# A two-term VectorE exponential, fixed PSUM slots, column-tiled FFN matmuls and a new planner in an attention-plus-FFN kernel

## The chip, the cores and the metric

The kernel runs on one core of a Trainium2 chip. A core has TensorE (PE: matmuls, with weight loads shown apart as PEld), VectorE (DVE), ScalarE (ACT), GpSimd (POOL), SyncE (SP, which here issues DMAs) and 16 DMA engines. Matmuls write into PSUM, which has 8 banks of 128 partitions x 512 fp32 values; TensorE reads its operands from SBUF. The metric is the device time of one execution in microseconds. For the kernel before it is 923.64 us, the median of 3 runs (923.12 to 926.92).

## The reference

The input x has 2048 tokens of 512 features in bf16. It is normalised, and the normalised xn goes through two branches:

```
xn = layernorm(x)                              # 2048 x 512
q = xn @ wq   (32 heads of 16)                 # 2048 x 512
k, v = xn @ wk, xn @ wv                        # one k and one v of 2048 x 16 for all heads
s = softmax(q k^T / 4) v, all heads, @ wo      # 2048 x 512
g = silu((silu(xn @ w_gate) * (xn @ w_up)) @ w_down)   # inner width 1792
out = x + s * g
```

The heavy part is the softmax: 32 heads x 2048 queries x 2048 keys give 134 million exponentials.

## The kernel before

**Tiles.** Heads are taken in 4 groups of 8 (`NQ`), and queries in 4 chunks of 512 (`NSC`). A *pair* is one group of heads on one query chunk: 16 pairs. Of a pair's 8 heads, 4 are computed in one *block* (`half` 0 or 1): 32 blocks. A block goes over 16 key tiles of 128 keys (`NT`), and each key tile is split in two *score tiles* (x = 0, 1) of two heads each. So there are 1024 score tiles, each 128 keys x 1024 (2 heads x 512 queries) in fp32: two PSUM banks.

**Scores.** A score tile is two matmuls (L771 to L776) with 32 contraction rows each; x = 0 uses row groups 0 and 1 of the array, x = 1 uses 2 and 3. They go into one of three slots of two banks, `ring[0..2]` (L338; `ring_96` to `ring_98` in the profile). Any slot serves either engine; the planner takes the one that comes free first (L757 to L769).

**Exponentials.** Most tiles go to ScalarE: one activation from the slot into a bf16 buffer `Pb` (L793; 8 buffers). Some go to VectorE, two tiles at a time, which builds the exponential from the bits of a fixed-point sum: a first pass from the slot to 16-bit integers `Ub` (L824, once per tile), then on both tiles together a mask for the mantissa `Wb` (L836), a mask for the exponent `Eb` (L839), a product Wb x Wb (L842) and a product Wb x Ub (L845). Three terms, `Eb`, `Ub` and `Wb`, each weighted by its own copy of v (`VD`, three copies), add up to the probability.

**PV.** Probabilities times v go into the one bank `o_ps` (L665), as four matmuls on the four 32-column groups of the array: one group of four for two ScalarE tiles (L813), three groups for a VectorE pair (L849 to L852). v carries a column of ones, so the sums of the softmax come out too. At the end of a block VectorE copies `o_ps` to SBUF (L708); four small DMAs, a reciprocal (L633), two DMAs and a product on GpSimd (L644) normalise a pair.

**FFN.** Everything else on TensorE goes through the one bank `m_ps`, as full 128 x 128 matmuls: per query chunk 14 column blocks with 4 gate matmuls (L563), a tanh on ScalarE (L568), silu on VectorE (L570), 4 up matmuls, and a product on VectorE (L574); then 4 token tiles of 14 down matmuls (L583) with a tanh (L589) and a product (L591). So do the q projections of later pairs (`g_q`, L547) and the output projections (`g_out`, L613).

**The order of the work.** The builder plans it in Python with a list scheduler (`_Sched`, L177 to L266) that holds a cost for each operation, a latency of 0.13 us between engines and 0.09 us for a change of the array's tile shape. The loop at L737 goes over key tiles in order; for each it fixes the slots and which tile, if any, VectorE takes (only while its planned backlog is under 4.0 us, `D_BL`, L751 to L755), adds the operations, and steps the plan until the scores are placed. FFN, q and output jobs join at fixed tile counts (`gates`, L680 to L691) with matmuls in bundles of two. In the end all operations are emitted by planned start, chained in that order on every engine (`chain`, L477; L869 to L872). The first part (statistics, normalisation, transposes, k and q of the first 512 tokens, L456 to L472) stands ahead of the plan and is not chained; k and v of tokens 512 to 2047 (`g_prolog`, L526) are in the plan. After the last block come the output projection of the last chunk and a check of ranges (L874 to L903).

Of the kernel before, what the change touches and what calls it, by code (L numbers as in the profile page):

```python
# [9 lines left out]
BF16 = mybir.dt.bfloat16  # L10
# [16 lines left out]
CE, CS, CM = 0.45803766, 0.46571725, 4.0 * 0.07629173  # L27
DEN_LO = 16.0
DEN_HI = 1e30
V_HI = 60000.0  # L30

# [135 lines left out]
class _Op:  # L167
    __slots__ = ("eng", "dur", "deps", "emit", "mode", "prio", "name", "start", "end", "left", "users", "ready", "seq")
# [8 lines left out]
class _Sched:  # L177
    LAT = 0.13
    SWITCH = 0.09
    SAME = {"DVE": 0.08, "POOL": 0.08}  # L180
    GUARD = {"PE": 2.0, "DVE": 0.2}

    def __init__(self, t0):
        self.free = {"PE": t0, "ACT": t0, "DVE": t0, "POOL": t0, "DMA": 0.0}
        self.ready = {e: [] for e in self.free}
        self.done = []
        self.seq = 0
        self.mode = None
        self.last_pe = None
        self.backlog = {e: 0.0 for e in self.free}  # L190

    def add(self, op):
        op.seq = self.seq
        self.seq += 1
        self.backlog[op.eng] += op.dur
        op.left = 0
        for d in op.deps:
            if d.start is None:
                d.users.append(op)
                op.left += 1  # L200
# [3 lines left out]

    def _arm(self, op):
        r = 0.0
        for d in op.deps:
            lat = self.LAT if d.eng != op.eng else self.SAME.get(op.eng, 0.0)
            r = max(r, d.end + lat)
        op.ready = r  # L210
        self.ready[op.eng].append(op)

    def _sw(self, o):
        return self.SWITCH if o.eng == "PE" and self.mode is not None and o.mode[0] != self.mode else 0.0

    def _pick(self, e):
# [3 lines left out]
        t = self.free[e]  # L220
        if e == "DMA":
            op = min(lst, key=lambda o: (o.ready, o.seq))
            return op.ready, op
        tm = max(t, min(o.ready for o in lst))
        best = min((o for o in lst if o.ready <= tm + 1e-9), key=lambda o: (o.prio, o.seq))
        if e in self.GUARD:
            hot = [o for o in lst if o.prio[0] <= 0 and o.ready > tm]
            if hot and best.prio[0] > 0:
                h = min(hot, key=lambda o: (o.ready, o.seq))
                lim = h.ready + self.GUARD[e]  # L230
                fit = [o for o in lst if o.ready <= tm + 1e-9 and tm + o.dur + self._sw(o) <= lim]
# [3 lines left out]
    def step(self):  # L235
        cand = None
        for e in self.free:
            c = self._pick(e)
# [698 lines left out]
```

## Time and profile before

| what | value |
|---|---|
| median of 3 runs | 923.64 us (923.12 to 926.92) |
| span of the profiled execution | 922.9 us |
| TensorE busy | 787.4 us (85%) in 5769 matmuls |
| VectorE busy | 709.9 us (77%) in 849 instructions |
| ScalarE busy | 822.8 us (89%) in 920 instructions |
| GpSimd busy | 58.1 us (6%) |
| mean granted TensorE clock | 0.914 |
| first exponential on ScalarE starts | 20.77 us |

All rows but the first are of the one profiled execution, whose own time from first to last instruction is 922.9 us. A group or timeline row reads: start and duration in us (or the group's busy time and the mean ns of one), engine, line, operation, output<-inputs by the program's names, shapes, and how many; square brackets hold the engine's idle time just before and what ended it. Instructions on one engine overlap at their ends, so the cost of one in a full queue is the distance from its start to the next start, not its duration. The granted clock is 1.0 or 0.5 at any one time.

### The profile page before, as it was taken

The numbers are of one execution on the slowest core, as the hardware profiler recorded it, in microseconds if no ns is written. First come the engines' busy times: TensorE is split into PE (matmuls) and PEld (weight loads), VectorE is DVE, ScalarE is ACT, GpSimd is POOL, SyncE is SP. The second block draws the span as 40 slices with busy tenths as digits, with TensorE's granted clock in tenths as the row PEclk, the third lists the DMA queues.
The fourth block names the chain that finished last, engine by engine and source line by source line (L and its number), as shares of the span: only waits on it lengthen the run. The fifth ranks groups of instructions, "written<-read, shape, count | busy, mean of one in ns | idle before, by whom it ended". The sixth has DMA issues, their size and how long they took to land.

```text
span 922.9 us, 14837 instructions
## 1 busy us (share of the span) xinstructions
PE 787.4 (85%) x5769; PEld 231.2 (25%) x5769; DVE 709.9 (77%) x849; ACT 822.8 (89%) x920; POOL 58.1 (6%) x64
## 2 busy tenths in 40 slices
PE   3799888889989898889989888898988889999960
PEld 1222222222222222222222222222222222222210
DVE  6426798887777768898879889888788778697763
ACT  2688899999899999999999999999999999899850
POOL 2100000000000110000001010000000020000001
PEclk9856799899799999999999999989999999799775
DMA  9100000000000000000000000000000000000001
GB/s 332 46 1 1 19 1 20 1 1 19 1 20 7 28 9 1 20 2 19 1 19 8 19 18 1 20 1 19 1 19 7 10 27 1 19 2 19 1 4 41
DMA packets 20110, 18.64 MB, mean 20 GB/s; under 512 B 9024, under 2 KB 15936, under 8 KB 20032
## 3 DMA queue, kind: packets, MB, share of 16 engines
q1 hardware_dynamic: 18448, 17.05, 6.1%
q8 instruction: 47, 0.77, 0.3%
q10 hardware_dynamic: 1584, 0.56, 0.2%
q14 instruction: 31, 0.25, 0.1%
HBM read 12.88 MB, written 2.36 MB: 17 GB/s over the span
## 4 chain that ended last, share of the span: by engine, by line
PE 43%; ACT 25%; DVE 19%; issue 8%; DMA 3%; SPq 2%; POOL 0%; ACTq 0%; DVEq 0%; POOLq 0%
PE o_ps L665 11%; PE m_ps L563 7%; PE ring_98 L772 6%; PE ring_97 L772 6%; PE ring_96 L772 5%; DVE Ub_129 L824 4%; PE m_ps L583 4%; DVE Ub_130 L824 4%; ACT Pb_125 L793 3%; ACT Pb_126 L793 3%; ACT Pb_122 L793 3%; ACT Pb_128 L793 3%; ACT Pb_121 L793 3%; ACT Pb_124 L793 3%; ACT Pb_123 L793 3%
## 5 line engine op out<-in xcount | busy, mean ns | idle before, releaser
L772 PEld LDWEIGHTS <-KT_84 32*128 32x128 bf16 x1024 | 51.0, 92 | 193.9 <-issue 186.9
L772 PEld LDWEIGHTS <-KT_85 32*128 32x128 bf16 x1024 | 50.3, 92 | 181.5 <-issue 179.1
L563 PE MATMUL m_ps<-xnT,wg_sb 128*128 128x512 bf16 x224 | 70.1, 415 | 5.4 <-DVE hT L574 2.0
L563 PE MATMUL m_ps<-xnT,wu_sb 128*128 128x512 bf16 x224 | 69.5, 404 | 4.0 <-DVE ab_137 L570 2.4
L583 PE MATMUL m_ps<-wd_sb,hT 128*128 128x512 bf16 x224 | 67.7, 391 | 5.5 <-DVE g_sb L591 5.4
L824 DVE TENSOR_SCALAR Ub_129<-ring_98 128x1024 uint16<-128x1024 f32 x37 | 45.2, 1223 | 31.9 <-PE ring_98 L772 28.3
L665 PEld LDWEIGHTS <-VA 128*32 128x32 bf16 x1684 | 42.9, 94 | 106.5 <-issue 106.2
L824 DVE TENSOR_SCALAR Ub_129<-ring_97 128x1024 uint16<-128x1024 f32 x38 | 46.5, 1223 | 24.9 <-PE ring_97 L772 16.3
L842 DVE TENSOR_TENSOR Wb_134<-Wb_134 128x2048 f16<-128x2048 f16 x45 | 58.7, 1305 | 0.0
L845 DVE TENSOR_TENSOR Wb_133<-Wb_133,Ub_129 128x2048 f16<-128x2048 f16 x46 | 57.9, 1259 | 0.8
L842 DVE TENSOR_TENSOR Wb_133<-Wb_133 128x2048 f16<-128x2048 f16 x46 | 57.1, 1240 | 0.0
L845 DVE TENSOR_TENSOR Wb_134<-Wb_134,Ub_130 128x2048 f16<-128x2048 f16 x45 | 55.8, 1240 | 0.7
L793 ACT ACTIVATE Pb_121<-ring_96 128x1024 bf16<-128x1024 f32 x39 | 42.7, 1095 | 10.4 <-PE ring_97 L772 8.6
L824 DVE TENSOR_SCALAR Ub_130<-ring_97 128x1024 uint16<-128x1024 f32 x33 | 40.3, 1222 | 13.4 <-PE ring_97 L772 6.1
L824 DVE TENSOR_SCALAR Ub_130<-ring_98 128x1024 uint16<-128x1024 f32 x30 | 36.7, 1222 | 17.5 <-PE ring_98 L772 13.3
L793 ACT ACTIVATE Pb_121<-ring_98 128x1024 bf16<-128x1024 f32 x35 | 38.3, 1094 | 9.4 <-PE ring_96 L772 7.7
L568 ACT ACTIVATE th_135<-m_ps 128x512 f32<-128x512 f32 x56 | 37.3, 667 | 9.3 <-PE m_ps L563 9.3
L824 DVE TENSOR_SCALAR Ub_130<-ring_96 128x1024 uint16<-128x1024 f32 x27 | 33.0, 1221 | 15.8 <-PE ring_96 L772 9.1
L793 ACT ACTIVATE Pb_128<-ring_97 128x1024 bf16<-128x1024 f32 x40 | 43.9, 1098 | 0.9 <-PE ring_97 L772 0.8
L665 PE MATMUL o_ps<-Pb_121,VA 128*32 128x512 bf16 x212 | 44.4, 416 | 0.3 <-ACT Pb_121 L793 0.3
L665 PE MATMUL o_ps<-Pb_128,VA 128*32 128x512 bf16 x210 | 44.4, 419 | 0.3 <-DVE oa_139 L708 0.2
L665 PE MATMUL o_ps<-Pb_127,VA 128*32 128x512 bf16 x210 | 44.4, 419 | 0.0
(161 smaller groups left out, 2097.3 us busy)
## 6 DMA issues: line engine op xcount, KB each, us to landing
rb_142<-dscr_147 SPq DMA_DIRECT2D x8, 256.0 KB
rb_142<-dscr_148 SPq DMA_DIRECT2D x8, 256.0 KB
wg_sb<-in_B_w_gate_dram SPq DMA_DIRECT2D x1, 1792.0 KB
wu_sb<-in_B_w_up_dram SPq DMA_DIRECT2D x1, 1792.0 KB
wd_sb<-in_B_w_down_dram SPq DMA_DIRECT2D x1, 1792.0 KB, 19.0
x_sb<-in_A_x_dram SPq DMA_DIRECT2D x3, 512.0 KB
oa_138<-oa_139 SPq DMA_DIRECT2D x32, 32.0 KB, 2.0
oa_140<-oa_141 SPq DMA_DIRECT2D x32, 32.0 KB, 2.0
```

Of the source, the lines that this page charges most:

```text
L563: return lambda: [nc.tensor.matmul(out=m_ps[:], lhsT=w[:, kc, f * P:(f + 1) * P], rhs=xnT[:, kc, sc * 512:(sc + 1) * 512], start=(kc == 0) ...
L568: t_ = OP("ACT", 0.48, [a], lambda: nc.scalar.activation(out=th[i][:], in_=m_ps[:], func=ACT.Tanh, scale=0.5), (0,), name="tanh")
L583: return lambda: [nc.tensor.matmul(out=m_ps[:, :D], lhsT=hT[:, f, tt * P:(tt + 1) * P], rhs=wd_sb[:, f, :], start=(f == 0), stop=(f == FC ...
L665: r.append(nc.tensor.matmul(out=o_ps[GRP * g:GRP * g + GRP, :], lhsT=lhs, rhs=rhs, start=(n == 0), stop=(n == pv_total[(b, g)] - 1), tile_ ...
L772: return [nc.tensor.matmul(out=ring[sl][:, u * 512:(u + 1) * 512], lhsT=KT[half][GRP * g:GRP * g + GRP, t * P:(t + 1) * P], rhs=QB[pair % ...
L793: ex = OP("ACT", 0.905, [scs[x], pdep, prev_exp], lambda i=i, sl=sl: nc.scalar.activation(out=Pb[i][:], in_=ring[sl][:], func=ACT.Exp, sca ...
L824: pa = OP("DVE", 1.16, [scs[dx], udep], lambda ui=ui, x=dx, sl=sl: nc.vector.tensor_scalar(out=Ub[ui][:, x * 1024:(x + 1) * 1024], in0=rin ...
L842: e3 = OP("DVE", 1.18, [e1], lambda ei=ei: nc.vector.tensor_tensor(out=Wb[ei][:].bitcast(FP16), in0=Wb[ei][:].bitcast(FP16), in1=Wb[ei][:] ...
L845: e4 = OP("DVE", 1.18, [e3], lambda ui=ui, ei=ei: nc.vector.tensor_tensor(out=Wb[ei][:].bitcast(FP16), in0=Wb[ei][:].bitcast(FP16), in1=Ub ...
```

## The change

- **VectorE's exponential has two terms.** The product Wb x Wb is gone, as is the term `Ub`; `Wb` is the mantissa mask times `Ub`, weighted by a new constant. Per pair of tiles VectorE does two first passes, two masks and one product, and PV takes two groups of four matmuls, each waiting only for its own term. `VD` holds two copies of v.
- **Slots are fixed.** `ring[0]` and `ring[1]` serve ScalarE alone, `ring[2]` VectorE alone. When a ScalarE tile is placed and VectorE's slot is free within 0.1 us (`MERGE`), VectorE's next tile, on the other two row groups, is placed right behind it (planned cost 0.015 us). ScalarE's and VectorE's tiles of a block need not come in key order; the last 9 tiles of a block (`D_LIM`) are not given to VectorE, which may take tiles of the next block instead.
- **FFN, q and output matmuls are column tiles.** Each 128 x 128 matmul becomes four of 128 x 32 (`cmm`) on the four column groups, the shape of the PV matmuls. Each contraction step is one operation of the plan (before: bundles of two, and of two down steps).
- **One event-driven plan.** The plan advances by events: `pe_pick` chooses for TensorE between a ScalarE tile, a ready group and a VectorE tile alone; a group goes ahead of a ScalarE tile only if it ends within 0.12 us (`TOL`) of the time at which the tile could start. Among groups, PV of finished blocks (or with 5 or more exponentials outstanding) comes first, then the start's matmuls, then VectorE's PV, then FFN, q and output groups, then ScalarE's PV. On VectorE the FFN operations come ahead of the first pass. Costs and latencies are new.
- **The start is in the plan, and chained.** Statistics, normalisation, transposes and the first k and q (in halves of 256 columns, with q's copy on ScalarE) have places in the order. 20 matmuls on constant data (`NWARM`) stand first on TensorE. The copy of k's weights stands first on GpSimd.

The diff, cut to its core:

```diff
-CE, CS, CM = 0.45803766, 0.46571725, 4.0 * 0.07629173
+CE, CW = 0.66858732, 0.66372796 * 1.0
+NWARM = 20
+D_START, D_LIM, D_LIM_END = 26, 9, 6
+F_ON, F_OFF = 30, 24
+PB_URG = 5
+TOL, MERGE = 0.12, 0.1
...
 class _Sched:
-    LAT = 0.13
-    SWITCH = 0.09
+    LAT = {"PE": 0.205, "ACT": 0.166, "DVE": 0.13, "POOL": 0.16, "DMA": 0.0, "EXT": 0.0}
+    SAME = {"PE": 0.0, "ACT": 0.0, "DVE": 0.03, "POOL": 0.05, "DMA": 0.0}
+    SWITCH = 0.105
+    HOT = 0.3
...
+    for i in range(NWARM):
+        chain("PE", nc.tensor.matmul(out=ring[2][:, 512:1024], lhsT=ident_bf[:], rhs=Pb[0][:, 0:512],
+                                     start=True, stop=True))
...
+    def cmm(dst, w, rhs, start, stop):
+        return [nc.tensor.matmul(out=dst[GRP * j:GRP * j + GRP, :], lhsT=w[:, GRP * j:GRP * j + GRP], rhs=rhs,
+                                 start=start, stop=stop, tile_position=(0, GRP * j)) for j in range(P // GRP)]
...
+    def grp_pe(parts, deps=()):
+        last = None
+        for emit in parts:
+            last = OP("PE", MMF, [m_rel[0], last] + list(deps), emit, (2,), "c", "fill")
+        return last
...
-        splits = [range(0, KC // 2), range(KC // 2, KC)] if KC > 1 else [range(KC)]
-        a = grp_pe([(mm(wg_sb, ks), len(ks) * MMF, []) for ks in splits], (2,))
+        def mm(w, kc):
+            return lambda: cmm(m_ps, w[:, kc, f * P:(f + 1) * P], xnT[:, kc, sc * 512:(sc + 1) * 512],
+                               kc == 0, kc == KC - 1)
+        a = grp_pe([mm(wg_sb, kc) for kc in range(KC)])
...
+    def act_sc(i, b, x, start):
+        sc, t = place_sc(i, b, x, start, MMF)
...
+        ex = OP("ACT", 0.904, [sc, pb_rel[k - NPB] if k >= NPB else None, cur["exp"]],
+                lambda: nc.scalar.activation(out=Pb[pi][:], in_=ring[i][:], func=ACT.Exp, scale=escale, bias=ebias),
+                (1,), name="exp")
+        cur["exp"] = ex
+        slot[i] = ex
...
+    def dve_sc(b, x, start, dur):
+        sc, t = place_sc(2, b, x, start, dur)
...
+        pa = OP("DVE", 1.135, [sc, wop_rel[u - NU] if u >= NU else None],
+                lambda: nc.vector.tensor_scalar(out=Ub[ui][:, x * 1024:(x + 1) * 1024], in0=ring[2][:], scalar1=ubias,
+                                                scalar2=UINF, op0=ALU.add, op1=ALU.min), (1.5, u), name="passA")
+        slot[2] = pa
...
-                e3 = OP("DVE", 1.18, [e1], lambda ei=ei: nc.vector.tensor_tensor(
-                    out=Wb[ei][:].bitcast(FP16), in0=Wb[ei][:].bitcast(FP16), in1=Wb[ei][:].bitcast(FP16),
-                    op=ALU.mult), (2, s), name="dQ")
+        o3 = OP("DVE", 1.1, [o1, o2], lambda: nc.vector.tensor_tensor(
+            out=Wb[ei][:].bitcast(FP16), in0=Wb[ei][:].bitcast(FP16), in1=Ub[ui][:].bitcast(FP16), op=ALU.mult),
+            (2, u, 2), name="dW")
...
+            def rank(o):
+                if o.name in ("pv", "dpv"):
+                    fin = ba is None or o.prio[1] < ba
+                    if fin or outst >= PB_URG:
+                        return (0, o.prio)
+                    return (1 if o.name == "dpv" else 3, o.prio)
+                if o.mode == "f":
+                    return (0.5, o.prio)
+                return (2, (o.seq,))
...
+        if tm is not None:
+            if ts is None or tm + sd.switch(co.mode) + co.dur <= ts + TOL:
+                cands.append(tm)
...
+    def pe_do(start, what):
...
+        if d_ok() and slot[2].start is not None and sd.avail(slot[2], "PE") <= start + MERGE:
+            x = act_x(b)
+            dt = dve_tile(1 - x)
...
+        act_sc(i, b, x, start)
+        dt = dve_tile(1 - x)
+        if dt is not None and tile_ready(*dt) is not None:
+            at = max(sd.free["PE"], sd.avail(slot[2], "PE"))
+            dve_sc(dt[0], dt[1], at, 0.015 if dt[1] != x else MMF)
```

More of the change, by code (lines that the diff above doesn't have):

```diff
@@ L511, in grp_pe, with pro_mm @@
+    def pro_mm(deps, bk, w, t0, t1, pr):
         last = None
[L512 to L524 removed]
@@ L869 @@
+    assert cur["issued"] == NTILE and job["f"] == len(ffn_list), (cur, job)
+    assert not [o for lst in sd.ready.values() for o in lst]
     order = sorted(sd.done, key=lambda o: (o.start, o.seq))
```

814 lines of the change are left out of this document (455 added, 359 removed).

## The prediction

> **What bounds the kernel now.** I read the cores view, then the page's busy shares, then stretches of the span by clock, then the timeline of a stretch in the middle, and last the two ends.
>
> ```profile
> core 0: 922.9 us, clock 0.914
> ```
>
> ```profile
> PE 787.4 (85%) x5769; PEld 231.2 (25%) x5769; DVE 709.9 (77%) x849; ACT 822.8 (89%) x920; POOL 58.1 (6%) x64
> ```
>
> Three engines are at 77 to 89% and none at 100%. The stretches (us, then PE, PEld, DVE, ACT and POOL busy with instruction counts, then clock) say why:
>
> ```profile
> 20.00:70.00 50.00, 42.17 (x284) 13.77 (x283) 17.24 (x43) 36.17 (x39) 6.75 (x18) 0.74 0.14 43
> 100.00:890.00 790.00, 705.69 (x5267) 206.14 (x5263) 647.88 (x721) 754.67 (x844) 43.49 (x27) 0.94 0.04 11
> 470.60:474.00 3.40, 1.83 (x12) 0.57 (x11) 2.49 (x5) 3.17 (x4) 0.00 (x0) 1.00 0.16 33
> 474.00:477.40 3.40, 3.40 (x22) 0.62 (x20) 2.37 (x3) 2.43 (x3) 0.00 (x0) 0.50 0.22 67
> 610.50:730.00 119.50, 105.89 (x833) 32.57 (x830) 100.55 (x110) 117.52 (x133) 6.23 (x4) 1.00 0.04 10
> ```
>
> The same view for the exponentials of ScalarE (line 793), and then for VectorE's first pass (line 824), in a stretch at full clock and one at half clock:
>
> ```profile
> 610.50:730.00 119.50, 114.34 (x123) 1.00 0.04 10
> 788.00:801.70 13.70, 9.24 (x10) 0.50 0.12 32
> ```
>
> ```profile
> 610.50:730.00 119.50, 32.99 (x27) 1.00 0.04 10
> 788.00:801.70 13.70, 2.45 (x2) 0.50 0.12 32
> ```
>
> Of ScalarE's counts I take one off each, the exponential that was already running. Full clock: (122 + 27)/119.5 = 1.247 score tiles per us. Half clock: (9 + 2)/13.7 = 0.80, that is 0.64 of the full rate. The mean of 0.94 over 100 to 890 us is 12% at half clock, so the whole stretch runs at 1.247 x (1 - 0.12 x 0.36) = 1.193. Check: 39 tiles are done by 70 us; the other 985 take 826 us, to 896. The last PV matmul stands here:
>
> ```profile
> 894.04 0.40 PE L665 MATMUL o_ps<-Wb_133,VD 128*32 128x512 f16 x4
> ```
>
> So this account (start, rate, clock, and a tail of 922.9 - 894.0 = 28.9 us) reproduces the kernel to 2 us, and I use it for the changed one.
>
> What sets the full-clock rate? ScalarE, in order of time:
>
> ```profile
> 401.74 1.03 ACT L793 ACTIVATE Pb_128<-ring_98 128x1024 bf16<-128x1024 f32 x1
> 402.65 1.04 ACT L793 ACTIVATE Pb_121<-ring_97 128x1024 bf16<-128x1024 f32 x1
> 403.55 0.62 ACT L568 ACTIVATE th_135<-m_ps 128x512 f32<-128x512 f32 x1
> 404.03 1.06 ACT L793 ACTIVATE Pb_122<-ring_96 128x1024 bf16<-128x1024 f32 x1
> ```
>
> Start to start an exponential costs (403.55 - 401.74)/2 = 0.905 us and a tanh 0.48 (the durations overlap). In the full-clock stretch, 122 of one and the remaining 10 of the other make 115.2 of 119.5 us: ScalarE is 96% full, so it binds whenever the clock is whole. VectorE is 84% busy there.
>
> **The change, part by part.**
>
> *VectorE's exponential.* Its rows, start to start:
>
> ```profile
> 398.84 1.22 DVE L824 TENSOR_SCALAR Ub_130<-ring_96 128x1024 uint16<-128x1024 f32 x1
> 399.99 0.68 DVE L574 TENSOR_TENSOR hT<-ab_137,m_ps 128x512 bf16<-128x512 f32 x1
> 400.58 1.22 DVE L824 TENSOR_SCALAR Ub_130<-ring_96 128x1024 uint16<-128x1024 f32 x1
> 401.83 0.69 DVE L836 TENSOR_SCALAR Wb_134<-Ub_130 128x2048 uint16<-128x2048 uint16 x1
> 402.44 0.69 DVE L839 TENSOR_SCALAR Eb_132<-Ub_130 128x2048 uint16<-128x2048 uint16 x1
> 403.04 1.22 DVE L842 TENSOR_TENSOR Wb_134<-Wb_134 128x2048 f16<-128x2048 f16 x1
> 404.21 0.69 DVE L570 SCALAR_TENSOR_TENSOR ab_136<-th_135,m_ps 128x512 f32<-128x512 f32 x1
> ...
> 406.63 1.23 DVE L824 TENSOR_SCALAR Ub_129<-ring_98 128x1024 uint16<-128x1024 f32 x1 [0.59 <-PE ring_98 L772]
> ```
>
> First pass 1.15, FFN operation 0.59, the two masks 0.61 and 0.60, a product 1.17. A pair of tiles now costs 2 x 1.15 + 0.61 + 0.60 + 2 x 1.17 = 5.85 us; one product goes, leaving 4.68, or 2.34 per tile. VectorE's other work between the ends is 187 operations of 0.6 (56 silu, 56 hT, 16 g2, 12 output products, 15 q, 32 copies of o_ps) and 16 reciprocals: about 116 us, 0.155 of a 750 us body. With this engine 95% full it takes (0.95 - 0.155)/2.34 = 0.340 tiles per us; it now takes 27/119.5 = 0.226. I take 95% because the backlog limit of 4.0 us, which turned tiles away, is gone. The one slot must refill in time: score start to VectorE's start is 406.63 - 406.12 = 0.51 (the TensorE row is below), plus the pass, 1.15, plus some 0.5 until ScalarE's next tile takes it along: 2.2 us against 1/0.340 = 2.9. It fits.
>
> *TensorE.* Its rows:
>
> ```profile
> 401.90 0.39 PE L772 MATMUL ring_97<-QB_119,KT_85 32*128 32x512 bf16 x2
> 401.91 0.39 PE L772 MATMUL ring_96<-QB_119,KT_85 32*128 32x512 bf16 x2
> 402.23 0.61 PE L563 MATMUL m_ps<-xnT,wg_sb 128*128 128x512 bf16 x2
> ...
> 406.12 0.39 PE L772 MATMUL ring_98<-QB_119,KT_85 32*128 32x512 bf16 x2
> 406.44 0.40 PE L665 MATMUL o_ps<-Eb_132,VD 128*32 128x512 f16 x4
> 406.67 0.39 PE L665 MATMUL o_ps<-Ub_130,VD 128*32 128x512 f16 x4
> 406.88 0.39 PE L665 MATMUL o_ps<-Wb_134,VD 128*32 128x512 f16 x4
> ```
>
> Two tiles on different row groups start 0.01 apart, so a joined one is free. Groups of four column tiles follow at 0.22. From one tile shape to another it is 0.32, so a change of shape costs 0.10. With some 250 tiles on VectorE the new body has 775 score starts, 388 PV groups of ScalarE's tiles, 250 of VectorE's (two terms instead of three) and 780 FFN, q and output groups: 2193 x 0.22 = 483 us, plus at most two changes per score start, 155 us. That is 638 of 750, 85%, with FFN groups now standing beside PV groups without a change. Priced as four column tiles, an FFN group stays at 0.22: the f16 groups above have its very shape. The bounds: 0.10 less where a change is saved, 0.11 more where four weight loads show.
>
> The weight loads of those three groups take 0.34 us for twelve, 0.11 for four:
>
> ```profile
> 406.44 0.34 PEld L665 LDWEIGHTS <-VD 128*32 128x32 f16 x12 [0.23 <-issue]
> ```
>
> They lie inside the 0.22 here, beside the matmuls.
>
> [...]
>
> *Fixed slots.* ScalarE keeps two. Rows 401.74 and 402.65 alternate between slots 98 and 97 while VectorE holds 96, at 0.91, so two suffice. A refill takes the 0.51 to the reader plus the notice of the release, an estimate of at most the 0.29 that the 0.51 has beyond its 0.22 of streaming: 0.80 of 0.905. I price it at nothing while TensorE comes within 0.1 us, half a group. I take ScalarE at 97%: with 72 x 0.48 = 35 us of tanh, (0.97 - 0.046)/0.905 = 1.021 tiles per us. Full-clock rate: 1.361.
>
> *The clock.* The 470.6 row has TensorE 1.83 of 3.4 us busy, and the next row stands at half clock. Groups per us rise from the denser tiles, so thin stretches should be fewer; I take 5.5% at half clock (bounds 0 and today's 12%): 1.361 x 0.98 = 1.334.
>
> [...]
>
> *Small edits at nothing.* GpSimd, 6% busy, copies k's weights before its fills, so the fills and one identity wait for that DMA; nothing reads them before the first PV group, and the first rstd follows at its time. The reciprocal yields to more of VectorE's queue, which delays the normalisation inside the next pair of blocks, some 45 us long. SyncE's queue keeps its order. Without that cover each would cost its own length, under 1 us.
>
> *The start.*
>
> ```profile
> 6.38 0.73 POOL L400 TENSOR_TENSOR rstd<-veps,neg_half 128x2 f32<-128x2 f32 x1 [1.68 <-DVE mv L394]
> ...
> 12.48 0.40 DVE L403 TENSOR_SCALAR xn_115<-x_sb,mv,rstd 128x512 bf16<-128x512 bf16 x1
> ...
> 20.77 1.02 ACT L793 ACTIVATE Pb_121<-ring_96 128x1024 bf16<-128x1024 f32 x1 [5.13 <-PE ring_97 L772]
> ```
>
> rstd is there at 7.1, but the normalisation waits on VectorE behind later chunks' statistics until 12.5. The written order takes 5.4 us off, and halves of 256 columns with q's copy on ScalarE some 3 more: 12.4. Against that stand 20 warm-up groups ahead of the first transpose: at half clock (0.43) 8.6 us from about 1.5, to 10.1, so up to 3 us late. I take 14 (bounds 12 and 18). The next 26 tiles are ScalarE's alone, 23.5 us, instead of the starved 20 to 70 us, where ScalarE ran 39 operations.
>
> *The sum.* 14 + 23.5 + (1024 - 26)/1.334 = 748 + 2 at the end, where VectorE takes no more tiles, + 28.9 = 816.4 us of span. The median of the runs is 0.7 above this span: 817.
>
> **The rivals.**
>
> *The one bank m_ps binds.* FFN, q and output groups pass through it one job after another:
>
> ```profile
> L574 DVE TENSOR_TENSOR hT<-ab_137,m_ps x2: 676/676/677, 400.0 to 417.6; 128x512 bf16<-128x512 f32 x2
> ```
>
> Every second FFN column block uses this ab buffer, so the 17.6 us from first to last are two blocks, 8.8 each: 56 make 493. A down block has 14 groups to 8, estimated 14: 224. With 27 jobs of about 3 that is 798 from tile 30, at 41 us: end 839 + 29 = 868 if no job gets shorter. For it: the jobs stand nearly end to end today. Against: FFN groups now rank above the PV of ScalarE's tiles on TensorE and ahead of the first pass on VectorE, which shortens the waits inside a job. If they give back a third of the excess, 850.
>
> *VectorE takes no more tiles than now*, because the refill is late: 1.021 + 0.226 = 1.247, x 0.98: 817 us of body, 886. Against: the 2.2 us above.
>
> *The weight loads show* on the FFN's 780 groups: 86 us more for TensorE, 724 of 750. Between hidden (817) and all on the path (903), half: 860. Against: the three groups at 0.22.
>
> *No half clock at all.* 998/1.361 = 733 instead of 748: 802. Against: thin stretches as at 470.6, which ends of blocks will still make.
>
> *Slower: late refills starve the two slots.* TensorE keeps its order, so a joined score matmul that waits for VectorE's slot holds every score matmul, PV and FFN group behind it. The clock then falls as well. With tanh taking 4.6%, ScalarE's period p must bring (0.954/p + 0.34) x 0.98 down to 998/855 = 1.167 to end at 923: p = 1.12, or 0.21 us lost on every tile, one group beyond the slack. From there on it is slower; with two groups, 0.44, it is 1040. For: an 85% TensorE has little room. Against: groups are now released singly, not two by two as in row 402.23.
>
> **How the numbers follow.** Forecast 0.62 (795 to 840), no half clock 0.06, m_ps 0.17, no more tiles 0.06, weight loads 0.02, starved slots 0.05, and 0.02 for something that I do not see, at about no change. The range: below, ScalarE 98.5%, VectorE 97% and no half clock give a rate of 1.387 and, starting at 12, 787; above, the m_ps case, 862. A difference within 0.5% (4.6 us) is about what a measurement of this kernel cannot tell from none: 0.02. Faster 0.93, slower 0.05.
>
> **What would show it.** Right: about 775 exponentials and 125 pairs; one product per pair; FFN groups at 0.22; first exponential near 14; ScalarE at 96% or more in full-clock stretches; half clock on under 8% of the body. Wrong: ScalarE idle before many exponentials with a score matmul as releaser; VectorE waiting for score tiles; FFN still running when the last PV stands.

## The result and the profile after

The changed kernel takes 828.62 us (median of 4 runs, 825.23 to 838.65) against 924.38 us for the kernel before (4 runs on the same chip, 923.12 to 926.92). The ratio is 0.893, 95% interval 0.889 to 0.898; it leaves out the longest run, whose mean clock was lower (0.944 against 0.955 to 0.962). The profiled execution has a span of 823.4 us.

The cores view and the page's busy shares of the changed kernel:

```profile
core 0: 823.4 us, clock 0.962
```

```profile
PE 732.8 (89%) x7965; PEld 223.0 (27%) x7965; DVE 756.7 (92%) x940; ACT 754.2 (92%) x850; POOL 52.1 (6%) x59
```

Its costliest groups (line, engine, operation, tiles, count | busy us, mean ns | idle time before them and what ended it). The last two are the FFN's gate and up matmuls:

```profile
L833 ACT ACTIVATE Pb<-ring 128x1024 bf16<-128x1024 f32 x770 | 727.8, 1099 | 26.0 <-PE ring L784 24.0
L860 DVE TENSOR_SCALAR Ub<-ring 128x1024 uint16<-128x1024 f32 x254 | 309.3, 1218 | 12.5 <-PE ring L784 5.2
L877 DVE TENSOR_TENSOR Wb<-Wb,Ub 128x2048 f16<-128x2048 f16 x127 | 155.4, 1223 | 0.0
L459 PE MATMUL m_ps<-xnT,wg_sb 128*32 128x512 bf16 x896 | 77.3, 388 | 4.2 <-DVE hT L594 3.3
L459 PE MATMUL m_ps<-xnT,wu_sb 128*32 128x512 bf16 x896 | 76.3, 392 | 5.0 <-DVE ab L590 4.2
```

VectorE now takes 254 of the 1024 score tiles instead of 182, with one product per pair. ScalarE and VectorE hardly wait for scores: 24.0 and 5.2 us in all.

Stretches of the changed kernel (us; PE, PEld, DVE, ACT, POOL busy with counts; clock, DMA share, GB/s), then the same middle stretch for ScalarE's exponentials alone and for VectorE's first pass alone:

```profile
20.00:45.00 25.00, 24.57 (x155) 8.30 (x154) 14.70 (x39) 18.92 (x19) 3.65 (x8) 0.50 0.28 89
45.00:70.00 25.00, 22.21 (x246) 7.59 (x244) 21.52 (x26) 22.90 (x27) 0.81 (x3) 0.95 0.01 2
100.00:700.00 600.00, 546.36 (x6024) 160.47 (x6023) 579.00 (x676) 587.23 (x661) 35.51 (x24) 0.99 0.05 13
```

```profile
100.00:700.00 600.00, 572.45 (x609) 0.99 0.05 13
```

```profile
100.00:700.00 600.00, 251.41 (x208) 0.99 0.05 13
```

The kernel before, same stretch, same three views:

```profile
100.00:700.00 600.00, 534.06 (x4024) 157.68 (x4020) 497.36 (x554) 576.06 (x646) 33.26 (x20) 0.96 0.04 11
```

```profile
100.00:700.00 600.00, 558.15 (x592) 0.96 0.04 11
```

```profile
100.00:700.00 600.00, 163.70 (x134) 0.96 0.04 11
```

With one taken off each count (the instruction already running), ScalarE and VectorE do (608 + 207)/600 = 1.358 tiles per us instead of (591 + 133)/600 = 1.207. VectorE's 0.345 against 0.222 is most of that. The better clock (0.99 against 0.96, some 2% of the stretch at half instead of 8%) is a small part: at the prediction's price, 0.36 of the rate lost at half clock, it is worth 2% of the rate, about 0.03 of the 0.151, an estimate. Both engines are over 96% busy there, so the middle of the kernel is full.

The two ends of the changed kernel are less full. First ScalarE's first exponentials, then VectorE's first one, then the last product with V and the last product of the FFN's down projection:

```profile
15.45 2.85 ACT L833 ACTIVATE Pb<-ring 128x1024 bf16<-128x1024 f32 x3 [0.88 <-PE ring L784]
18.81 2.11 ACT L833 ACTIVATE Pb<-ring 128x1024 bf16<-128x1024 f32 x2 [0.50 <-PE ring L784]
21.41 2.11 ACT L833 ACTIVATE Pb<-ring 128x1024 bf16<-128x1024 f32 x2 [0.48 <-PE ring L784]
...
49.75 1.23 DVE L860 TENSOR_SCALAR Ub<-ring 128x1024 uint16<-128x1024 f32 x1 [1.30 <-PE ring L784]
```

```profile
790.99 0.40 PE L677 MATMUL o_ps<-Wb,VD 128*32 128x512 f16 x4
...
794.37 3.21 PE L459 MATMUL m_ps<-wd_sb,hT 128*32 128x512 bf16 x56 [0.17 <-DVE g_sb L607]
...
805.62 4.63 PE L459 MATMUL m_ps<-wd_sb,hT 128*32 128x512 bf16 x56 [0.96 <-DVE g_sb L607]
```

After the first three, each pair of exponentials waits half a microsecond for TensorE, which is busy for 24.57 of 25 us at half clock. At the end three more down blocks follow the last product with V.

### The profile page after: what moved, and what is told of

The parts are those of the page before. It is cut to its first block, busy times and chain, and to the rows that moved or that the text cites. A ratio compares the mean times of both kernels' runs of the same rounds, so it can differ in the third digit from the quotient of the medians.

```text
span 823.4 us, 19256 instructions
## 1 busy us (share of the span) xinstructions
PE 732.8 (89%) x7965; PEld 223.0 (27%) x7965; DVE 756.7 (92%) x940; ACT 754.2 (92%) x850; POOL 52.1 (6%) x59
## 4 chain that ended last, share of the span: by engine, by line
DVE 54%; PE 20%; ACT 13%; issue 7%; DMA 2%; SPq 2%; DVEq 0%; POOL 0%; ACTq 0%; POOLq 0%
DVE Ub L860 21%; ACT Pb L833 11%; DVE Wb L877 10%; PE ring L784 7%; DVE Wb L872 6%; PE m_ps L459 6%; DVE Eb L875 5%; PE o_ps L677 4%; DVE hT L594 3%; DVE ab L590 3%; SPq L700 2%; DVE oa L689 2%; ACT th L588 2%; DMA dn<-oa 1%; DVE ab L621 1%
## 5 line engine op out<-in xcount | busy, mean ns | idle before, releaser
L833 ACT ACTIVATE Pb<-ring 128x1024 bf16<-128x1024 f32 x770 | 727.8, 1099 | 26.0 <-PE ring L784 24.0
L784 PE MATMUL ring<-QB,KT 32*128 32x512 bf16 x2048 | 325.8, 390 | 41.1 <-ACT Pb L833 24.7
L860 DVE TENSOR_SCALAR Ub<-ring 128x1024 uint16<-128x1024 f32 x254 | 309.3, 1218 | 12.5 <-PE ring L784 5.2
L784 PEld LDWEIGHTS <-KT 32*128 32x128 bf16 x2048 | 93.6, 91 | 332.2 <-issue 326.6
L677 PE MATMUL o_ps<-Pb,VA 128*32 128x512 bf16 x1540 | 156.2, 396 | 0.4 <-DVE oa L689 0.4
L877 DVE TENSOR_TENSOR Wb<-Wb,Ub 128x2048 f16<-128x2048 f16 x127 | 155.4, 1223 | 0.0
L872 DVE TENSOR_SCALAR Wb<-Ub 128x2048 uint16<-128x2048 uint16 x127 | 88.8, 700 | 0.7
L875 DVE TENSOR_SCALAR Eb<-Ub 128x2048 uint16<-128x2048 uint16 x127 | 88.0, 693 | 0.0
L459 PE MATMUL m_ps<-xnT,wg_sb 128*32 128x512 bf16 x896 | 77.3, 388 | 4.2 <-DVE hT L594 3.3
L459 PE MATMUL m_ps<-xnT,wu_sb 128*32 128x512 bf16 x896 | 76.3, 392 | 5.0 <-DVE ab L590 4.2
```

The lines of the kernel that those rows point to most:

```text
L459: return [nc.tensor.matmul(out=dst[GRP * j:GRP * j + GRP, :], lhsT=w[:, GRP * j:GRP * j + GRP], rhs=rhs, start=start, stop=stop, tile_posi ...
L677: r.append(nc.tensor.matmul(out=o_ps[GRP * g:GRP * g + GRP, :], lhsT=lhs, rhs=rhs, start=(n == 0), stop=(n == pv_total[(b, g)] - 1), tile_ ...
L784: return lambda: [nc.tensor.matmul(out=ring[sl][:, u * 512:(u + 1) * 512], lhsT=KT[half][GRP * g:GRP * g + GRP, t * P:(t + 1) * P], rhs=QB ...
L833: lambda: nc.scalar.activation(out=Pb[pi][:], in_=ring[i][:], func=ACT.Exp, scale=escale, bias=ebias),
L860: lambda: nc.vector.tensor_scalar(out=Ub[ui][:, x * 1024:(x + 1) * 1024], in0=ring[2][:], scalar1=ubias, scalar2=UINF, op0=ALU.add, op1=AL ...
L872: o1 = OP("DVE", 0.55, [pa, pa0, w_rel[u - NE] if u >= NE else None], lambda: nc.vector.tensor_scalar(out=Wb[ei][:], in0=Ub[ui][:], scalar ...
```

## The experiments

My theory after the result was: (1) both of the engines that take exponentials are filled, by the shorter exponential and by the slots; (2) what is left over lies at the start, where TensorE runs at half clock, and at the end, behind the FFN's one bank. Rivals were that one part alone carries the gain, or that the clock does. Ratios are to the kernel before, run beside each kernel.

**The two-term exponential, taken back out and put in alone.** The first run is the changed kernel with the old exponential:

```diff
+        oq = OP("DVE", 1.1, [o1, o2], lambda: nc.vector.tensor_tensor(
+            out=Wb[ei][:].bitcast(FP16), in0=Wb[ei][:].bitcast(FP16), in1=Wb[ei][:].bitcast(FP16), op=ALU.mult),
+            (2, u, 2), name="dQ")
...
-        for i, (buf, o, rel) in enumerate(((Eb[ei], o2, e_rel), (Wb[ei], o3, w_rel))):
+        for i, (buf, o, rel) in enumerate(((Eb[ei], o2, e_rel), (Ub[ui], o3, wop_rel), (Wb[ei], o3, w_rel))):
```

> The changed kernel with the three-term exponential put back: a second product on VectorE per pair and a third PV group, everything else as changed. Theory (VectorE's cost per tile sets how many tiles it takes, ScalarE is full either way): a tile costs 2.93 us instead of 2.34, so at 97% busy VectorE takes (0.97 - 0.155)/2.93 = 0.278 tiles per us instead of 0.345, the body runs at 1.29 instead of 1.357 tiles per us, some 108 pairs instead of 127, and the time is about 866 us (plus 38). Rival (the plan and the fixed slots bring the gain, VectorE's cost does not bind): no more than 8 us slower than the changed kernel, under 838 us.

Measured: 864.12 us, ratio 0.930 (0.922 to 0.939); VectorE takes 214 tiles. As the theory said.

The second is the kernel before with the two-term exponential and nothing else of the change:

```diff
-CE, CS, CM = 0.45803766, 0.46571725, 4.0 * 0.07629173
+CE, CW = 0.66858732, 0.66372796 * 1.0
...
-                       for i, buf in enumerate((Eb[ei], Ub[ui], Wb[ei])) for g in range(4)]
+                       for i, buf in enumerate((Eb[ei], Wb[ei])) for g in range(4)]
```

> The kernel before with the two-term exponential alone: one product less per pair, two PV groups, the old planner, slots and full-width matmuls. Theory: VectorE keeps its share of time (0.66 us of each us for tiles), takes 0.66/2.34 = 0.282 tiles per us instead of 0.226, full-clock rate 1.30, with today's 12% at half clock 1.247: 70 + 790 + 29 = 890 us, 34 less than before. Rival (the old planner's backlog limit and shared slots hold the rate, so cheaper tiles only leave VectorE idle): within 8 us of 924.

Measured: 901.69 us, ratio 0.973 (0.964 to 0.982): between the theory's 890 and the rival's 916, so neither holds as it stands. VectorE takes 210 tiles instead of 182, but its row, from the grouped view of that run, shows what stops it:

```profile
L824 DVE TENSOR_SCALAR Ub<-ring 128x1024 uint16<-128x1024 f32 x210 | 256.1, 1221 | 112.1 <-PE ring L772 83.5 <-ACT Pb L793 22.4 <-ACT th L568 3.9
```

It idles 112.1 us ahead of the first pass, mostly for score tiles, against 12.5 us in the changed kernel. So the shorter exponential is worth about 27 us in the old plan (928.93 - 901.69) and 36 in the new one (864.12 - 828.62, from two chips); the larger share of the 96 us, about 65 (928.93 - 864.12), is the plan with its slots, joining and prologue. No run splits these 65 us among them: undoing the fixed slots or the joining, as below, loses more than the whole plan gained.

**The column tiles, undone.** Each group of four column tiles becomes one matmul over the whole array, in the same order of the plan:

```diff
-        return [nc.tensor.matmul(out=dst[GRP * j:GRP * j + GRP, :], lhsT=w[:, GRP * j:GRP * j + GRP], rhs=rhs,
-                                 start=start, stop=stop, tile_position=(0, GRP * j)) for j in range(P // GRP)]
+        return [nc.tensor.matmul(out=dst[:, :], lhsT=w, rhs=rhs, start=start, stop=stop)]
```

> The changed kernel in the same order on every engine, with each group of four column tiles of the FFN, q and output matmuls replaced by one full 128x128 matmul. Theory (a change of tile shape costs 0.10 us and TensorE has some 100 us to spare): about 280 places where an FFN group follows or precedes a PV group gain a change, 28 us more on TensorE, of which part is on the path: 832 to 845 us. Rival 1 (weight loads of column tiles cost): faster than the changed kernel, under 822. Rival 2 (TensorE's slack takes it all): within 3 us of the changed kernel, 826 to 832.

Measured: 827.91 us, ratio 0.886 (0.877 to 0.896). No difference that can be measured, within the 1% of that interval: neither the saved changes of shape nor four weight loads instead of one show in the time, and the 832 to 845 us of the theory didn't come.

**The warm-ups at the start, left out** (they compute nothing of the output):

```diff
-NWARM = 20
+NWARM = 0
```

> The changed kernel without the 20 warm-up matmuls. Theory: they end 1 us after the first normalised tile is ready and hold the clock up only to 16.7 us, so without them the first transpose starts about 1 us earlier and the first matmuls run at half clock: first exponential at 15 to 16.5 us, time within 3 us of the changed kernel. Rival (the warm clock carries the start): first exponential 3 us or more later, 831 or more.

Measured: 833.05 us, ratio 0.895 (0.887 to 0.903). The time is where the rival has it (831 or more), but the interval takes in the changed kernel's ratio, and the first exponential comes at 16.74 instead of 15.45 us, 1.3 later and not 3. What the warm-ups are worth isn't measured.

**The backlog limit of the kernel before, doubled.** I had given the end of this limit as the reason why VectorE would fill.

```diff
-    D_START, D_BL = 20, 4.0
+    D_START, D_BL = 20, 8.0
```

> The kernel before with one constant changed: VectorE's backlog limit of 4.0 us becomes 8.0; the exponential keeps its three terms. It tests a reason of my prediction, that this limit and not VectorE's speed kept VectorE from taking more tiles in the kernel before, where VectorE was idle for a good part of the time. Theory A (the limit held it back): between 100 and 700 us the pass on VectorE goes from 0.223 to about 0.26 tiles per us, the time falls by 15 to 30 us to 895 to 910. Rival B (something else holds it back: the slots of the ring that both engines share, or the order of the plan): VectorE's rate stays within 0.01 of 0.223 and the time stays within 8 us of 924.

Measured: 1223.11 us, ratio 1.322 (1.311 to 1.333). Neither theory. The groups and the waits of this run:

```profile
L793 ACT ACTIVATE Pb<-ring 128x1024 bf16<-128x1024 f32 x728 | 702.2, 1036 | 394.2 <-PE ring L772 381.0
...
L824 DVE TENSOR_SCALAR Ub<-ring 128x1024 uint16<-128x1024 f32 x296 | 358.1, 1218 | 97.5 <-PE ring L772 31.9
```

```profile
PE ring L772 <- DVE Ub L824: 138.9, 151, 2.8
```

VectorE does get to 0.262 tiles per us between 100 and 700 us, as theory A had it, but ScalarE falls from 0.985 to 0.610: it waits 381.0 us for score tiles. With a longer backlog, tiles that VectorE will only read later stand in slots that ScalarE needs, and TensorE, which keeps its order, waits 151 times for VectorE to empty one. The limit did not hold VectorE back for nothing; it protected the shared slots. The mean clock of that stretch is 0.77 against 0.96, and how much of the loss goes with the clock and how much with the slots the run doesn't tell.

**The fixed slots, undone in the changed kernel.** Both engines take the slot that comes free first:

```diff
-        rel = [i for i in (0, 1) if slot[i].start is not None]
+        rel = [i for i in (0, 1, 2) if slot[i].start is not None]
...
-    def dve_sc(b, x, start, dur):
-        sc, t = place_sc(2, b, x, start, dur)
+    def dve_sc(b, x, start, dur, j):
+        sc, t = place_sc(j, b, x, start, dur)
```

> The changed kernel with the fixed slots undone: both engines take whichever of the three slots comes free first, as in the kernel before; VectorE still has one score tile at a time, and the joining stays. Theory A (VectorE needs a slot of its own to be refilled in time): ScalarE takes a third tile whenever VectorE's slot comes free alone, VectorE waits for score tiles, its rate over 100 to 700 us falls from 0.345 to below 0.32 tiles per us, and the time rises to 840 to 880. Rival B (what counts is that VectorE's next tile is started as soon as its last is read, whichever slot it stands in): VectorE's rate stays within 0.01, time within 8 us of the changed kernel.

Measured: 1179.19 us, ratio 1.279 (1.270 to 1.289). The direction was theory A's, the size was not:

```profile
L833 ACT ACTIVATE Pb<-ring 128x1024 bf16<-128x1024 f32 x1024 | 973.1, 1079 | 79.1 <-PE ring L784 75.9
```

ScalarE computes all 1024 tiles and VectorE none. In the new plan ScalarE's choice is made first, so without a slot kept for it VectorE never finds one. This shows that the fixed slot is what gives VectorE its tiles under this plan's rule; what another rule of sharing would give, it does not show. The middle stretch has one more surprise:

```profile
100.00:700.00 600.00, 558.85 (x3968) 116.47 (x3967) 76.67 (x116) 536.47 (x589) 20.66 (x17) 0.63 0.03 9
```

With one consumer less, TensorE stands at a mean clock of 0.63, and ScalarE doesn't even keep its own pace of 0.905 us per tile: 600/588 is 1.02. At its own pace, 1024 tiles (927 us) and 72 tanh (35) between a start of 15 and a tail of 30 would end at about 1007 us, an estimate. So some 170 of the 350 us lost against the changed kernel come with the low clock, and the rest with VectorE's missing tiles.

**The joining, undone.** VectorE's tile is taken from the same two heads as ScalarE's, so that the two use the same rows of TensorE and run after each other: in this run two of them in a row last 0.61 us (at 400.18 us) and a lone one 0.39 (at 401.09), where a joined pair of the changed kernel lasts 0.40 (at 400.65). In the code:

```diff
-            dt = dve_tile(1 - x)
+            dt = dve_tile(x)
...
-        x = act_x(b, 1 - dt[1])
+        x = act_x(b, dt[1])
         act_sc(i, b, x, start)
-        dt = dve_tile(1 - x)
+        dt = dve_tile(x)
```

> The changed kernel, with VectorE's score tile taken from the same two heads, and so the same row groups of TensorE, as the tile of ScalarE that it is joined to, instead of the other two. The two matmul groups then follow each other instead of running side by side; nothing else changes, though the plan orders itself anew around it. It tests the joining alone. Theory A (TensorE, busy for 732.8 of 823.4 us, has no room for it): up to 254 tiles times 0.22 us are 55 us more for TensorE, half to all of it on the path, time 850 to 880. Rival B (TensorE's idle time takes it, since ScalarE and VectorE bind): within 8 us of the changed kernel.

Measured: 895.60 to 994.36 us in four runs, median 941.33; their mean clocks go with their times, from 0.933 for the shortest to 0.802 for the longest, so no ratio with an interval is given. Two stretches of one run:

```profile
200.00:300.00 100.00, 95.96 (x990) 27.48 (x990) 94.79 (x109) 99.47 (x111) 8.84 (x6) 1.00 0.06 15
440.00:580.00 140.00, 140.00 (x866) 22.42 (x862) 85.22 (x94) 96.77 (x97) 6.91 (x5) 0.50 0.04 10
```

Theory A is right that TensorE has no room, but the loss is larger than it had and comes in two pieces. At full clock the scores go first and the FFN pays: by 350 us this run has started 445 score tiles and 864 FFN matmuls, the changed kernel 432 and 1000. Then the clock drops at 436 us and stays at half for 157 us with TensorE busy all through. The last product with V comes at 828.2 instead of 791.0 us, 37 later. By then 672 of the FFN's 2688 matmuls are still to do; they run through their one bank without scores beside them, at half clock for the most part (0.50 between 850 and 915 us), and the tail is 948.9 - 828.2 = 120.7 us, 88 longer. In this view of the tail the releasers name each other in turn:

```profile
863.30 0.60 ACT L588 ACTIVATE th<-m_ps 128x512 f32<-128x512 f32 x1 [5.46 <-PE m_ps L459]
863.93 0.69 DVE L590 SCALAR_TENSOR_TENSOR ab<-th,m_ps 128x512 f32<-128x512 f32 x1 [2.68 <-ACT th L588]
864.67 1.90 PE L459 MATMUL m_ps<-xnT,wu_sb 128*32 128x512 bf16 x16 [1.47 <-DVE ab L590]
866.62 0.69 DVE L594 TENSOR_TENSOR hT<-ab,m_ps 128x512 bf16<-128x512 f32 x1 [2.00 <-PE m_ps L459]
```

Why the clock doesn't come back in the middle, where TensorE is busy, its rows there suggest, groups 0.54 us apart:

```profile
499.93 0.62 PE L677 MATMUL o_ps<-Wb,VD 128*32 128x512 f16 x4
500.48 0.61 PE L784 MATMUL ring<-QB,KT 32*128 32x512 bf16 x2
501.02 0.62 PE L677 MATMUL o_ps<-Pb,VA 128*32 128x512 bf16 x4
```

Every matmul here uses a quarter of the array. Four of them side by side do the work of one pass of the full array, which takes (3.21 - 0.39)/13 = 0.217 us at full clock, by the row at 794.37 of the changed kernel (14 groups). A group of four and a lone score tile, which is half of that, are together 0.325 us of full-speed work in 2 x 0.54 us: 0.30. With the score tile joined to a second one it is 0.434 in the same time: 0.40. By the counts of the view above, the 866 matmuls from 440 to 580 us, at half clock, are 866 x 0.217/4 us in 140 us, 0.34 of what the array could do; the 990 from 200 to 300 us, at full clock, are 0.54. In the changed kernel's trace the clock changes in steps of 3.41 us. Adding up its matmuls in this way over windows of that length, with a matmul that crosses a border shared by time, its seven returns to full clock follow windows of 0.38 to 0.42, and the windows at half clock that are followed by half clock hold at most 0.36. (The 0.31 to 0.44 in the expectation further on counts each matmul whole in the window where it starts, which blurs the border.) So the joining is worth its 0.22 us per tile on TensorE, which has no room for them, and beyond that it makes the work denser, 0.40 against 0.30 here, enough for the clock to come back. That the density is the cause is my reading of these counts, which the last section extends to the kernel before and the next experiment tests; the half clock on a busy TensorE, the FFN that is left over and what both cost are shown.

**Filling the start.** If density sets the clock, added work should bring it back. One matmul of 256 columns through the full array behind each of the first 26 score tiles, into a place that nobody reads, and then two of them:

```diff
+        if cur["issued"] <= 26:
+            for _ in range(2):
+                fl = _Op("PE", 0.107, [], lambda: nc.tensor.matmul(out=ring[2][:, 256:512], lhsT=ident_bf[:],
+                                                                   rhs=wq_sb[:, 0, 0:256], start=True, stop=True),
+                         (0,), "c", "fl")
```

> The changed kernel, with one more matmul behind each of ScalarE's first score tiles up to the 26th: 256 columns through the full array into a part of the ring that nobody reads, so that the output is the same and only the work of TensorE rises. It tests why the first 26 tiles took 34.3 us where I had counted 23.5. Theory A (TensorE's clock stands at half from 16.7 to 47.4 us because little of the array is at work in each window of 3.41 us, 0.12 to 0.34 of what it could do, while the clock comes back elsewhere at 0.31 to 0.44): with about 0.08 more per window the clock comes back some windows sooner and the first pass on VectorE starts at 43 to 47 instead of 49.8. Rival B (the clock is fixed by something other than the amount of work): the clock stays at half up to about 47 us, each added matmul costs 0.21 us on a TensorE that is already busy all through, and the first pass on VectorE starts at 52 to 55.

> As the run with one added matmul behind each of the first 26 score tiles, with two of them (512 columns through the full array per tile, the output unchanged). Theory A (the amount of work in a window sets the clock): with about 0.16 more per window most windows pass 0.4, the clock comes back within one or two windows of the first exponential, and the first pass on VectorE starts at 41 to 45 instead of 49.8, sooner than with one added matmul. Rival B (it is not the amount of work): half clock up to about 47 us or longer, and the added 0.43 us per tile put the first pass on VectorE to 56 to 61.

Measured: 831.43 us, ratio 0.900 (0.893 to 0.908), and 833.26 us, 0.904 (0.899 to 0.909). The stretches of the first, then of the second:

```profile
20.00:45.00 25.00, 23.83 (x146) 8.94 (x142) 13.49 (x35) 13.93 (x15) 3.67 (x8) 0.50 0.27 86
45.00:70.00 25.00, 23.92 (x171) 6.75 (x175) 11.15 (x16) 17.12 (x18) 0.82 (x3) 0.58 0.00 1
```

```profile
20.00:45.00 25.00, 21.08 (x168) 9.06 (x166) 13.28 (x36) 13.66 (x15) 4.42 (x11) 0.80 0.28 88
45.00:70.00 25.00, 22.27 (x231) 7.59 (x230) 16.89 (x23) 21.90 (x25) 0.81 (x3) 1.00 0.01 2
```

With one matmul neither theory's figures came: the clock stays at half longer than before, to 66 us, and VectorE's first pass starts at 59.33. TensorE was full already (24.57 of 25 us without the added work), so the added work pushed other work out: from 16 to 45 us there are 36 score matmuls instead of 44, and all matmuls together, counted as above, are 0.33 of what the array could do, against 0.32 in the changed kernel. With two they are 0.41, and the clock does answer as theory A has it (0.80 instead of 0.50), but the first pass starts at 55.65, not at 41 to 45: the added matmuls and the reordered prologue stand ahead of the score tiles, and ScalarE starts 14 exponentials in 20 to 45 us instead of 18 (15 and 19 less the one already running). So in this run the clock came up with the added work, at a price above the gain. How fast the start would be at full clock without the added work stays open.

**The end.** The last three down products go to free halves of the score slots instead of the FFN's bank:

```diff
+        alt = n - (4 * NSC - 3) if n >= 4 * NSC - 3 and cur["issued"] == NTILE else -1
+        dn_ps = m_ps[:, :D] if alt < 0 else ring[alt][:, 512:512 + D]
...
-        a = grp_pe([lambda f=f: cmm(m_ps[:, :D], hT[:, f, tt * P:(tt + 1) * P], wd_sb[:, f, :], f == 0, f == FC - 1)
+        a = grp_pe([lambda f=f: cmm(dn_ps, hT[:, f, tt * P:(tt + 1) * P], wd_sb[:, f, :], f == 0, f == FC - 1)
```

> The changed kernel, with the last three down products of the FFN written to free halves of the ring (which holds no scores any more) instead of the one bank that all FFN jobs share. It tests whether the shared bank sets the end: in the changed kernel the down products of the last chunk follow the last product with V by some 19 us and the tail is 32.4 us where I had counted 28.9. Theory A (the bank sets the end): the tail from the last product with V falls by 2 to 5 us, to 27 to 30, and the time by as much, to 823 to 827. Rival B (the division by the row sums and its DMA, ahead of the FFN's first product, set the end): the tail stays within 1 us of 32.4 and the time within 2 us of the changed kernel's.

The last product with V, and the down products that now follow each other without waiting for a bank:

```profile
798.54 0.40 PE L682 MATMUL o_ps<-Wb,VD 128*32 128x512 f16 x4
...
800.27 9.25 PE L459 MATMUL ring<-wd_sb,hT 128*32 128x512 bf16 x168
```

The tail is 827.4 - 798.5 = 28.9 us, 3.5 less than 32.4. The control below has 32.3, so the bank does hold up the end; the run without column tiles keeps it and has 29.6, so it isn't alone in that. The whole run is at 826.70 us, ratio 0.891 (0.886 to 0.897), where a gain of 3.5 us can't be told from none. The same, with the FFN let in after 16 tiles, beside the changed kernel itself:

```diff
-F_ON, F_OFF = 30, 24
+F_ON, F_OFF = 16, 24
```

> The changed kernel with the last three down products in free halves of the ring, as in the run with end banks, and with the FFN let in after 16 tiles instead of 30. It tests whether the shared bank, occupied end to end from 41 to 812 us, sets the end, and is the version that I expect to be the quickest. Theory A: the FFN's last job comes some 10 us sooner, ahead of the last product with V; the tail is 27 to 30 us, the time 814 to 823. Rival B (the start, where TensorE is busy for 24.57 of 25 us at half clock, has no room for it): the first pass on VectorE comes 5 us or more later than 49.8 and the time is 825 to 835.

> The changed kernel itself, on the same chip as the other three runs, so that differences of 1% between them can be read against it. All theories: 0.888 to 0.898 of the kernel before.

Measured: 827.02 us (0.898, 0.892 to 0.905) and 830.21 us (0.899, 0.893 to 0.905). The control lies just above the 0.888 to 0.898 expected of it, so a difference of under 1% between runs on different chips means nothing here. VectorE's first pass starts at 50.1 us, so rival B's later start didn't come; the tail is 821.0 - 792.1 = 28.9, the last FFN product stands at 802.7 instead of 813.9 in the control, but it doesn't come ahead of the last product with V. A shorter tail shows in both profiles; a shorter time, such as the 814 to 823 us of theory A, isn't measured.

## Why the prediction was right, point by point

The forecast was 816.4 us of span, 817 of time; it came to 823.4 and 828.62, within the range of 787 to 862. (The upper end is called the m_ps case there, but that rival's own working gives 868 or 850.) The profiled run was the quickest of the four, so 3.4 us of the miss in time, from 825.23 to the median, are in no row below. The terms against the profile:

| term | predicted us | measured us |
|---|---|---|
| first exponential | 14 | 15.45 |
| first 26 tiles, to VectorE's first pass | 23.5 | 49.75 - 15.45 = 34.3 |
| body, to the last product with V | 748 + 2 | 790.99 - 49.75 = 741.2 |
| tail | 28.9 | 823.4 - 790.99 = 32.4 |

*Right: the body.* 254 tiles for VectorE (predicted 250), 0.345 per us (0.340), both engines over 96% busy, FFN groups 0.217 apart (0.22), and two slots that feed ScalarE: the slower rival, late refills, didn't come. The body is 9 us shorter than I had it because the clock stands at 0.99 between 100 and 700 us, 2.3% of it at half instead of my 5.5%: the forecast's own rate of 1.361 then becomes 1.361 x (1 - 0.023 x 0.36) = 1.350, and 998 tiles take 739 us instead of 748.

*Half right: why VectorE takes more tiles.* I wrote that "the backlog limit of 4.0 us, which turned tiles away, is gone". It did turn tiles away: doubled, it lets VectorE take 0.262 per us. But that made the kernel before 1.32 times as long, and in the new plan the shared slots left VectorE without a tile. As I read the two runs, what lets VectorE take more without starving ScalarE is that its tile no longer takes a slot from ScalarE; the limit was the kernel before's way of living without that. Fixed slots under the old plan were not run.

*Mis-sized: the start, +10.8 us.* I let ScalarE run 26 tiles at its own pace. The clock is at half from 16.7 to 47.4 us, and TensorE, with the scores and the rest of the prologue, needs all of 25 us there, so ScalarE waits. The rows of the kernel before held the warning: a clock of 0.74 from 20 to 70 us, and I priced those tiles without it. Even that was too good: its first clock record is at 30.3 us and the time ahead of it counts as full, but the score matmuls there last 0.61 us (at 21.84, say), as at half clock, against 0.39 at full.

*Mis-sized: the tail, +3.5 us.* I carried the old tail over. The rival in which the one bank binds was partly true: the FFN's last product comes after the last product with V, and taking the bank away from three down blocks gives the 3.5 us back. But the 850 to 868 us that this rival stood for didn't come: from the first FFN matmul at 51.6 us the jobs take 760 us, to 811.6, where it had 798 us from 41 on.

*Too small a role: the joining.* I priced the joined tile as free, and it is: in the rows below an FFN group follows 0.32 us after a lone score tile and 0.32 after a joined pair. I didn't price what it spares: undone, it costs over 60 us even in the shortest run (895.60), through FFN work put off to the end and a clock that stays at half. TensorE's 85% (89% in the end) left less room than I thought.

```profile
399.78 0.39 PE L784 MATMUL ring<-QB,KT 32*128 32x512 bf16 x2
400.10 0.61 PE L459 MATMUL m_ps<-wd_sb,hT 128*32 128x512 bf16 x8
400.65 0.40 PE L784 MATMUL ring<-QB,KT 32*128 32x512 bf16 x4
400.97 0.62 PE L459 MATMUL m_ps<-wd_sb,hT 128*32 128x512 bf16 x8
```

*No effect where I gave one: FFN groups beside PV groups "without a change".* The saving of 0.10 us per change may be there on TensorE; in the time it isn't (827.91 us without column tiles). Nor do the four weight loads of a group show there, which the rival on them had at 86 us of TensorE.

## What to carry to other kernels

Where two engines drain one pool of PSUM slots behind an engine that works in order, try giving each its own slots before you shift work from one to the other: in this kernel, raising the share of the slower one in the shared pool cost 32%. When a stretch runs at half clock, count how much of the array its matmuls fill per microsecond, not only how busy TensorE is: with the joining undone, quarter-array matmuls that filled 0.34 of the array stood at a clock of 0.50 for 140 us on a TensorE that was 100% busy. Price the first and the last stretch of a kernel from their own clock and their own queue, since a full middle leaves its errors there.

## What the runs showed of the hardware

The clock was the surprise. In the traces of the kernel before and the changed kernel it changes in steps of 3.41 us between 1.0 and 0.5, and idleness alone isn't what keeps it low: with the joining undone, TensorE was busy for 140.00 of 140 us at 0.50. What separates the two in my counts is how much of the array is at work. Count each matmul as its columns times the share of the array that it uses, at 0.217 us for 512 columns through the full array, and share one that crosses the border of two windows of 3.41 us by time. In these two traces together, the 65 windows that are followed by half clock then hold at most 0.38 of what the array could do; of the 434 that are followed by full clock, 430 hold 0.38 or more, and the other 4 lie between 0.37 and 0.38. The same bound serves for going down and for coming back. Counted without the share of the array, by columns alone, no bound does that: the best leaves 31 windows on its wrong side, against 2. Whole stretches of two experiments agree, by the counts of their views at a quarter of the array per matmul: 0.34 at a clock of 0.50 with the joining undone (440 to 580 us) and 0.36 at 0.63 with shared slots (100 to 700 us), against 0.54 at 0.99 in the changed kernel (100 to 700 us). By what rule the clock is granted, these counts don't show.

Gaps in TensorE's work do not separate the two. In the kernel before, no gap in the 3.41 us ahead of the drop at 788.04 us is over 0.30 us, while no drop follows its gap of 1.84 us at 261.86 us, nor the gap of 1.88 us at 466.16 us in the changed kernel; and the stretch from 440 to 580 us with the joining undone, which has no gap at all, stays at half.

A group of four column tiles takes here what one matmul of the full array takes. The row at 794.37 of the changed kernel gave 0.217 us for the group; the same block without column tiles is (3.19 - 0.39)/13 = 0.215 us for one matmul:

```profile
817.01 3.19 PE L459 MATMUL m_ps<-wd_sb,hT 128*128 128x512 bf16 x14
```
